# A longer GpSimd operation between slot writes, and gathered rows turned through the scratch in list order

## The chip, the core and the metric

The kernel runs on one NeuronCore of a Trainium2 chip. Its engines run beside each other, each with an instruction stream of its own: TensorE (PE in the rows; PEld is its weight load), VectorE (DVE), ScalarE (ACT), GpSimd (POOL) and SyncE (SP), which issues most of the DMAs. GpSimd issues the DMAs whose rows are picked by an index, gathers and scatters. The metric is device time in microseconds (us) of one execution, the median of several.

## What is computed

Windowed causal attention over 8 batches, 8 heads, 576 positions and head size 64, whose output rows are the input of a mixture of experts with the top 2 of 8 experts per row.

```python
scores = scale * q @ k.T                       # window of 64 positions, causal
attn = softmax(where(mask, scores, -1e9))
x = (attn @ v).transpose(0, 2, 1, 3).reshape(4608, 512)
noisy = x @ w_gate + log1p(exp(x @ w_noise)) * noise
top2 = the two largest of 8 per row; w = softmax over these two
for e in range(8):                             # rows whose top 2 holds e
    h = maximum(x[mask] @ w1[e], 0)            # 512 -> 1024
    out[mask] += w[mask, e] * (h @ w2[e])      # 1024 -> 512
```

## The kernel before

**Attention.** The 36 units `j` (128 rows each) run in one software pipeline, `for j in range(NT + 3)` (L719 to 769), in which the steps of neighbouring units are woven together by hand. Among them are `pv` (L324, 64 small matmuls of 64x85 per unit), the four transposes of `transp` (L301), and on GpSimd the softmax subtraction (L289). Each unit's output rows are stored to `X` (`xrows`) in DRAM.

**Routing.** After units 7, 14, 21, 27 and 36 a `route(c)` (L407) works out for the rows so far which two experts they go to and at which place of each expert's list. Then `scatter` (L481) writes, for each unit and each of the two choices, 128 entries of 8 bytes (row number, weight) to `L` (`slots`) in DRAM: one indirect DMA of GpSimd (L483). There are 72 of these slot writes. Ahead of each stands a one-element memset of `spacer` (L482). They are queued in the list `slots` and drained by `drain_slots` at fixed places of the program: one to three per unit within the attention loop, several at a time behind it.

**Experts.** For each expert `e` the list is cut into chunks of 384, 448 and 384 rows, `(e, c)`. `load_list` (L520) and `load_lists` (L532) read the lists back from `slots` with SP, once all slot writes ahead of them have landed. `gather` (L543) fetches the rows of a chunk with one indirect DMA per tile of 128 rows (L546, tile `xg`). `turn` (L564) brings them into the layout that TensorE needs, with the feature on the partition, and splits them into a high and a low part, `xh` (ACT, L584) and `xl` (DVE, L585). `up` (L609) multiplies by `w1` (L625 to 627, 96 matmuls per chunk) and `down` (L645) by `w2` (L654 to 656, 24 matmuls per tile); `add_rows` (L640) adds the weighted result to the output with an indirect DMA of GpSimd.

For expert 0 the turning is done by TensorE transposes (L579). For experts 1 to 7 it goes through a scratch `xs` in DRAM: per tile one DMA out (`turn_out`, L555, pieces of 128 values) and one back (`turn_in`, L560), each partition then holding 4 whole blocks of 128 values, and a 32x32 block transpose on DVE (L574) into `xy`. In `xy` the row number within a tile is laid out such that L584 and L585 read with a stride (`"p t k c -> p k c t"`) and write in sequence.

**What sets the order.** `spread` (L55) lays a list of side tasks evenly over the groups of matmuls of a chunk. The gather of the next chunk (`whole` for all tiles, then `turn_out` for all tiles, then `turn_in` for all tiles) is laid over `up` of the current one, the turn of the next chunk over `down` of the current one. Each engine and SP's queue run their instructions in this written order. The first matmuls of chunk (0, 0), `up00`, are issued ahead of time within the last units of the attention loop. Chunk (0, 1) is gathered after the first four routings, chunk (0, 2) after the last.

Of the kernel before, what the change touches and what calls it, by code (L numbers as in the profile page):

```python
# [8 lines left out]
F32 = mybir.dt.float32  # L9
# [5 lines left out]
OP = mybir.AluOpType  # L15
# [6 lines left out]
NT = NP * NB  # L22
# [13 lines left out]
W1G = 12  # L36
TURN = 33
AHEAD = 16
XB = 8
SLOTS = 5  # L40
WARM = 4

# [23 lines left out]
def tile_kernel(ctx, tc, qT, kT, vx, vT, wgx, noise, w1, w2, out):  # L66
    nc = tc.nc
# [68 lines left out]
    warm(10)  # L136
    ident = consts.tile([128, 128], F32)
    make_identity(nc, ident)
    spacer = consts.tile([1, 1], F32)
    zero = gw.tile([128, DM], F32, name="zero", bufs=1)  # L140
    nc.vector.memset(zero, 0.0)

# [264 lines left out]
    def route(c):  # L407
# [71 lines left out]
        yield lambda: nc.vector.reciprocal(w[:, 0, :, 1], sm)  # L479
        yield lambda: nc.vector.tensor_tensor(w[:, 1, :, 1], e, w[:, 0, :, 1], op=OP.mult)  # L480
        def scatter(c2, q):  # L481
            nc.gpsimd.memset(spacer, 0.0)  # L482
            s = nc.gpsimd.indirect_dma_start(  # L483
                out=L, out_offset=bass.IndirectOffsetOnAxis(ap=posi[:, c2, q:q + 1], axis=0),
                in_=val[:, c2, q, :], in_offset=None)
            for x in scattered:
                tc.declare_no_dep(s.ins, x.ins, reason="distinct slots")
            scattered.append(s)
# [21 lines left out]
    pending, slots = [], []  # L510


    LT, XG, XH, XL, HH = {}, {}, {}, {}, {}
    work = [(e, c) for e in range(E) for c in range(len(CHUNKS))]

    def tiles(c):
        return [(q, min(128, CHUNKS[c] - q * 128)) for q in range(-(-CHUNKS[c] // 128))]
# [25 lines left out]
    def gather(e, c):  # L543
        def whole(q, m):
            XG[e, c, q] = exa.tile([128, DM], F32, name="xg", bufs=XB)
            nc.gpsimd.indirect_dma_start(out=XG[e, c, q][:m], out_offset=None, in_=X[:DUMP + seen.get((e, c), NT) * 128],  # L546
                                         in_offset=bass.IndirectOffsetOnAxis(ap=LT[e, c][q][:m, 0:1], axis=0))
        if e == 0:
            return [lambda q=q, m=m: whole(q, m) for q, m in tiles(c)]

        b = {}

        def turn_out(q, m):
            b[q] = dram.tile([4, 128, 128], F32, name="xs", bufs=8)
            nc.sync.dma_start(b[q].rearrange("g p c -> (g p c)")[:m * DM].rearrange("(g p c) -> p g c", g=4, c=128),  # L555
                              XG[e, c, q][:m].rearrange("p (g c) -> p g c", g=4))

        def turn_in(q, m):
            XG[e, c, q] = exa.tile([128, DM], F32, name="xg", bufs=XB)
            nc.sync.dma_start(XG[e, c, q][:, :m * 4],  # L560
                              b[q].rearrange("g p c -> (g p c)")[:m * DM].rearrange("(p x) -> p x", p=128))
        return [lambda q=q, m=m, f=f: f(q, m) for f in (whole, turn_out, turn_in) for q, m in tiles(c)]

    def turn(e, c):  # L564
        pool = (exa, EXB.get("p"))[work.index((e, c)) % 2]
# [5 lines left out]
        def f(q, m):  # L571
            if e:
                y = exa.tile([128, m // 32, KD, 32], F32, name="xy", bufs=2)
                nc.vector.transpose(y.rearrange("p t k c -> p (t k c)"), XG[e, c, q][:, :m * 4])  # L574
                cur[q] = y.rearrange("p t k c -> p k c t")
            else:
                y = turn_bank()[:, :KD * m].rearrange("p (k m) -> p k m", k=KD)
                for k in range(KD):
                    nc.tensor.transpose(y[:, k], XG[e, c, q][:m, k * 128:k * 128 + 128], ident[:m, :m])  # L579
                cur[q] = y.rearrange("p k (c t) -> p k c t", c=32)  # L580

        def g(q, m):
            h, l = (x[:, :, q * 128:q * 128 + m].rearrange("p k (c t) -> p k c t", c=32) for x in (xh, xl))
            nc.scalar.activation(h, cur[q], AF.Copy)  # L584
            nc.vector.tensor_tensor(l, cur[q], h.bitcast(F32), op=OP.subtract)  # L585
        return [lambda q=q, m=m, x=x: x(q, m) for q, m in tiles(c) for x in (f, g)]
# [341 lines left out]
```

## Time and profile before

| | |
|---|---|
| median of 3 runs | 1135.25 us (1126.39 to 1136.22) |
| the profiled execution | 1131.99 us, its span 1130.2 us |
| PE busy | 1044.2 us (92%) |
| DVE, ACT, POOL busy | 469.2, 437.4, 338.6 us |
| slot writes, POOL L483 | 72, mean 972 ns |
| gathers, POOL L546 | 80; those of experts 1 to 7 mean 990 ns |

The profile is of one execution, with times from the start of the span. An engine's row has its start, its duration, the line, the operation, the tiles (written <- read) and in brackets how long the engine was idle ahead of it and what ended that. "issue" there means that the profile shows nothing that the engine waited for, "remote" that the releaser is not known. PEclk is the granted share of TensorE's full clock: 1.00 is 2.4 GHz and 0.50 is 1.2 GHz.

### The profile page before, as it was taken

To read this page: it belongs to the slowest core of one execution; us is meant where nothing else is said; L and a number is where in the kernel's file an instruction comes from. 1 tells how busy PE (TensorE), PEld (TensorE's weight loads), DVE (VectorE), ACT (ScalarE), POOL (GpSimd) and SP (SyncE) were. 2 spreads that over 40 slices of the span, in tenths; PEclk is the share of its full clock that TensorE was granted. 3 is DMA by queue.
4 is the path that set the end of the run, shared out by engine and by line. 5 is a ranking of instruction groups with operands and counts; after the bars stand their busy time and mean duration, and the time that the engine had idled before them with its cause. 6 is when DMAs were issued, how large, how long until landed. Compare 5 with 4: busy or idle time off the path is not lost. (4 is left out here: it accounts for less than half of the span.)

```text
span 1130.2 us, 19820 instructions
## 1 busy us (share of the span) xinstructions
PE 1044.2 (92%) x8025; PEld 925.7 (82%) x8025; DVE 469.2 (42%) x943; ACT 437.4 (39%) x1011; POOL 338.6 (30%) x387
## 2 busy tenths in 40 slices
PE   9788888578599999999999999999999999999996
PEld 8777777366589888898988898889888988889895
DVE  5586556324114523452263325334533452354320
ACT  4776555332123432442253335323432343253320
POOL 4345444616412222122312123212221222322121
PEclk9898888879699999999999999999999999999998
DMA  9988889537414752564447445634762564244422
GB/s 321 314 300 206 214 198 307 150 133 235 123 27 112 221 146 33 173 195 103 81 130 200 103 108 146 180 81 98 203 172 40 157 205 113 44 99 112 102 33 31
DMA packets 104519, 168.07 MB, mean 149 GB/s; under 512 B 15096, under 2 KB 50530, under 8 KB 102626
## 3 DMA queue, kind: packets, MB, share of 16 engines
q1 hardware_dynamic: 84962, 126.78, 35.3%
q0 software_dynamic: 19456, 39.93, 19.2%
q8 instruction: 65, 1.06, 0.4%
q14 instruction: 36, 0.29, 0.1%
HBM read 109.54 MB, written 57.14 MB: 147 GB/s over the span
## 5 line engine op out<-in xcount | busy, mean ns | idle before, releaser
L625 PE MATMUL ps_u<-xh,w1h 128*128 128x384 f32 (+1 forms) x752 | 261.6, 348 | 15.6 <-ACT xh L584 15.1
L640 POOL DMA_INDIRECT out_dram<-yo,lts x70 | 112.1, 1602 | 543.9 <-ACT yo L659 430.7
L626 PE MATMUL ps_u<-xl,w1h 128*128 128x384 f32 (+1 forms) x752 | 261.4, 348 | 4.5 <-DVE xl L585 4.5
L627 PE MATMUL ps_u<-xh,w1l 128*128 128x384 f32 (+1 forms) x752 | 260.3, 346 | 0.0
L654 PE MATMUL ps_d<-w2h,hh 128*128 128x512 f32 x576 | 225.3, 391 | 0.0
L656 PE MATMUL ps_d<-w2h,hl 128*128 128x512 f32 x576 | 225.2, 391 | 0.0
L655 PE MATMUL ps_d<-w2l,hh 128*128 128x512 f32 x576 | 225.0, 391 | 0.0
L632 DVE SCALAR_TENSOR_TENSOR hl<-ps_u,hh 128x384 fp32r<-128x384 f32 x188 | 104.8, 557 | 275.9 <-ACT hh L631 261.6
L631 ACT ACTIVATE hh<-ps_u 128x384 fp32r<-128x384 f32 x188 | 92.5, 492 | 246.9 <-PE ps_u L627 236.5
L625 PEld LDWEIGHTS ps_u<-xh,w1h 128*128 128x128 f32 x752 | 141.9, 189 | 23.9 <-ACT xh L584 18.7
L626 PEld LDWEIGHTS ps_u<-xl,w1h 128*128 128x128 f32 x752 | 141.9, 189 | 11.2 <-DVE xl L585 6.7
L627 PEld LDWEIGHTS ps_u<-xh,w1l 128*128 128x128 f32 x752 | 141.9, 189 | 4.0
L585 DVE TENSOR_TENSOR xl<-xy,xh 128x512 fp32r<-128x512 f32 (+1 forms) x70 | 71.5, 1021 | 150.7 <-ACT xh L584 150.7
L654 PEld LDWEIGHTS ps_d<-w2h,hh 128*128 128x128 f32 x576 | 108.6, 189 | 23.8 <-issue 1.8
L656 PEld LDWEIGHTS ps_d<-w2h,hl 128*128 128x128 f32 x576 | 108.4, 188 | 22.8
L655 PEld LDWEIGHTS ps_d<-w2l,hh 128*128 128x128 f32 x576 | 108.5, 188 | 21.9
L659 ACT ACTIVATE yo<-ps_d,lts 128x512 f32<-128x512 f32 x63 | 43.4, 690 | 160.2 <-PE ps_d L656 119.1
L324 PE MATMUL ps_o<-vw,pt 64*64 64x85 f32 x2176 | 71.0, 257 | 29.4 <-issue 22.8
L584 ACT ACTIVATE xh<-xy 128x512 fp32r<-128x512 f32 (+1 forms) x70 | 74.4, 1063 | 56.1 <-DVE xy L574 56.1
L324 PEld LDWEIGHTS ps_o<-vw,pt 64*64 64x64 f32 x2176 | 58.7, 149 | 40.3 <-issue 32.1
L483 POOL DMA_INDIRECT slots<-val,posi x72 | 70.0, 972 | 20.1 <-issue 14.7
L546 POOL DMA_INDIRECT xg<-xrows,lts x70 | 69.3, 990 | 21.4 <-issue 20.1
(149 smaller groups left out, 991.3 us busy)
## 6 DMA issues: line engine op xcount, KB each, us to landing
xs<-xg SPq DMA_DIRECT2D x63, 256.0 KB
xg<-xs SPq DMA_DIRECT2D x63, 256.0 KB
w2s<-in_w_dram SPq DMA_DIRECT2D x7, 2048.0 KB
w1s<-in_w_dram SPq DMA_DIRECT2D x7, 2048.0 KB
vw<-in_vx_dram SPq DMA_DIRECT2D x36, 272.0 KB
out_dram<-zero SPq DMA_DIRECT2D x37, 256.0 KB
qc<-in_qT_dram SPq DMA_DIRECT2D x36, 256.0 KB
KW<-in_kT_dram SPq DMA_DIRECT2D x36, 256.0 KB
```

The source lines that it names most:

```text
L324: nc.tensor.matmul(PO[j][u * 64:u * 64 + 64, a, g * 2 + x, :], lhsT=pt[pa, w, u * 2 + g, x * 64:x * 64 + 64], rhs=v[pa, (i + w) % 2, :, u, ...
L584: nc.scalar.activation(h, cur[q], AF.Copy)
L585: nc.vector.tensor_tensor(l, cur[q], h.bitcast(F32), op=OP.subtract)
L625: nc.tensor.matmul(p[:, :n], lhsT=w1h[:, k, fs], rhs=xh[:, k, :n], start=(k == 0), stop=False)
L626: nc.tensor.matmul(p[:, :n], lhsT=w1h[:, k, fs], rhs=xl[:, k, :n], start=False, stop=False)
L627: nc.tensor.matmul(p[:, :n], lhsT=w1l[:, k, fs], rhs=xh[:, k, :n], start=False, stop=(k == KD - 1))
L631: nc.scalar.activation(h, p[:, :main], AF.Relu)
L632: nc.vector.scalar_tensor_tensor(l, p[:, :main], 0.0, h.bitcast(F32), op0=OP.max, op1=OP.subtract)
L640: nc.gpsimd.indirect_dma_start(out=out[:DUMP + seen.get((e, c), NT) * 128], out_offset=bass.IndirectOffsetOnAxis(ap=LT[e, c][q][:m, 0:1], ...
L654: nc.tensor.matmul(p, lhsT=hh[f][:, sl], rhs=w2h[:, f, :], start=(f == 0), stop=False)
L655: nc.tensor.matmul(p, lhsT=hh[f][:, sl], rhs=w2l[:, f, :], start=False, stop=False)
L656: nc.tensor.matmul(p, lhsT=hl[f][:, sl], rhs=w2h[:, f, :], start=False, stop=(f == KF - 1))
```

## The change

Two parts. First, `spacer` grows to 256 values, and ahead of those slot writes that are issued from unit 34 on (`j < NT - 2` no longer holds), the one-element memset is replaced by an addition of 256 values on one partition, also on GpSimd. That concerns 39 of the 72 slot writes. Second, for experts 1 to 7 the gathered tiles go to the scratch `xs` as whole rows (2 KB each), the scratch is one tile per chunk, and it is read back by four DMAs per chunk, one for each group of 32 partitions, in pieces of 128 values, into one tile `xc` (one buffer). DVE's block transpose then gives `xy` in list order, and L584 and L585 (L588 and L589 of the change) read runs of 32 values. The pool `xg` shrinks from 8 buffers to 5, since the way back no longer uses it.

```diff
+PAUSE = 256
-XB = 8
+XB = 5
...
-    spacer = consts.tile([1, 1], F32)
+    spacer = consts.tile([1, PAUSE], F32)
...
         def scatter(c2, q):
-            nc.gpsimd.memset(spacer, 0.0)
+            if j < NT - 2:
+                nc.gpsimd.memset(spacer[:, 0:1], 0.0)
+            else:
+                nc.gpsimd.tensor_tensor(spacer, zero[0:1, :PAUSE], zero[0:1, :PAUSE], op=OP.add)
             s = nc.gpsimd.indirect_dma_start(
...
-        b = {}
+        b = dram.tile([WIDE, DM], F32, name="xs", bufs=3)
 
         def turn_out(q, m):
-            b[q] = dram.tile([4, 128, 128], F32, name="xs", bufs=8)
-            nc.sync.dma_start(b[q].rearrange("g p c -> (g p c)")[:m * DM].rearrange("(g p c) -> p g c", g=4, c=128),
-                              XG[e, c, q][:m].rearrange("p (g c) -> p g c", g=4))
-
-        def turn_in(q, m):
-            XG[e, c, q] = exa.tile([128, DM], F32, name="xg", bufs=XB)
-            nc.sync.dma_start(XG[e, c, q][:, :m * 4],
-                              b[q].rearrange("g p c -> (g p c)")[:m * DM].rearrange("(p x) -> p x", p=128))
-        return [lambda q=q, m=m, f=f: f(q, m) for f in (whole, turn_out, turn_in) for q, m in tiles(c)]
+            nc.sync.dma_start(b[q * 128:q * 128 + m], XG[e, c, q][:m])
+
+        def turn_in(g):
+            if g == 0:
+                XC[e, c] = exa.tile([128, WIDE // 32, 128], F32, name="xc", bufs=1)
+            nc.sync.dma_start(XC[e, c][32 * g:32 * g + 32, :CHUNKS[c] // 32],
+                              rows(b, g * 128, [[DM, 32], [32 * DM, CHUNKS[c] // 32], [1, 128]]))
+        return ([lambda q=q, m=m, f=f: f(q, m) for f in (whole, turn_out) for q, m in tiles(c)]
+                + [lambda g=g: turn_in(g) for g in range(4)])
...
-                nc.vector.transpose(y.rearrange("p t k c -> p (t k c)"), XG[e, c, q][:, :m * 4])
-                cur[q] = y.rearrange("p t k c -> p k c t")
+                nc.vector.transpose(y.rearrange("p t k c -> p (t k c)"), XC[e, c][:, q * 4:q * 4 + m // 32].rearrange("p t d -> p (t d)"))
+                cur[q] = y.rearrange("p t k c -> p k t c")
...
         def g(q, m):
-            h, l = (x[:, :, q * 128:q * 128 + m].rearrange("p k (c t) -> p k c t", c=32) for x in (xh, xl))
+            h, l = (x[:, :, q * 128:q * 128 + m].rearrange("p k (t c) -> p k t c", c=32) for x in (xh, xl))
```

GpSimd, the last units of the attention loop, before (`val`, `posi` are the entries and places of a routing; DMASW counts GpSimd's own DMAs):

```order
L483 DMA slots<-val_172,posi 38400x2 [waits DMASW2_49]
L482 MEMSET spacer 1x1 [waits Pool_49]
L483 DMA slots<-val_172,posi 38400x2 [waits DMASW3_49]
L289 TENSOR_TENSOR t<-t,mx 128x512 [waits DVE_49,Activation_49]
L482 MEMSET spacer 1x1 [waits Pool_49]
L483 DMA slots<-val_172,posi 38400x2 [waits DMASW4_49]
```

and the same place of the change:

```order
L487 DMA slots<-val_172,posi 38400x2 [waits DMASW2_49]
L484 MEMSET spacer 1x1 [waits Pool_49]
L487 DMA slots<-val_172,posi 38400x2 [waits DMASW3_49]
L290 TENSOR_TENSOR t<-t,mx 128x512 [waits DVE_49,Activation_49]
L486 TENSOR_TENSOR spacer<-zero 1x256 [waits Pool_49]
L487 DMA slots<-val_172,posi 38400x2 [waits DMASW4_49]
```

Nothing has moved on GpSimd; from this place on the memset's place is taken by the addition, 39 times. SP's queue, from the reading of the lists to the second chunk of expert 1, before:

```order
L535 DMA lts<-slots 64x7x2
L209 DMA w1s<-in_w_dram 128x4096
L555 DMA xs<-xg 128x4x128 x3
L560 DMA xg<-xs 128x512 x3
L209 DMA w1s<-in_w_dram 128x4096
L555 DMA xs<-xg 128x4x128 x3
L555 DMA xs<-xg 64x4x128
L560 DMA xg<-xs 128x512 x3
L560 DMA xg<-xs 128x256
L213 DMA w2s<-in_w_dram 128x4096
```

and of the change:

```order
L539 DMA lts<-slots 64x7x2
L210 DMA w1s<-in_w_dram 128x4096
L558 DMA xs<-xg 128x512 x3
L563 DMA xc<-xs 32x12x128 x4
L210 DMA w1s<-in_w_dram 128x4096
L558 DMA xs<-xg 128x512 x3
L558 DMA xs<-xg 64x512
L563 DMA xc<-xs 32x14x128 x4
L214 DMA w2s<-in_w_dram 128x4096
```

The places are the same; a chunk's way back is always four DMAs now, and each of them carries rows of all tiles of the chunk. DVE at the turn of chunk (1, 1), before (DMAHW counts SP's DMAs):

```order
L574 STREAM_TRANSPOSE xy<-xg 128x512 [waits DMAHW0_49]
L585 TENSOR_TENSOR xl<-xy,xh 128x4x128 [waits Activation_49]
L574 STREAM_TRANSPOSE xy<-xg 128x512 [waits DMAHW1_49]
L585 TENSOR_TENSOR xl<-xy,xh 128x4x128 [waits Activation_49]
L574 STREAM_TRANSPOSE xy<-xg 128x512 [waits DMAHW2_49]
```

and of the change:

```order
L578 STREAM_TRANSPOSE xy<-xc 128x512 [waits DMAHW3_49,DMAHW4_49,DMAHW2_49,DMAHW1_49]
L589 TENSOR_TENSOR xl<-xy,xh 128x4x128 [waits Activation_49]
L578 STREAM_TRANSPOSE xy<-xc 128x512
L589 TENSOR_TENSOR xl<-xy,xh 128x4x128 [waits Activation_49]
L578 STREAM_TRANSPOSE xy<-xc 128x512
```

The first transpose of a chunk now waits for all four loads, the others for none.

## Rows read from the trace of the kernel before

**Rows 1.** Stretches of 2 us and one of 100: length, busy time per engine, PEclk, DMA share, GB/s

```profile
228.00:230.00 2.00, 0.58 (x2) 0.18 (x2) 0.00 (x0) 0.00 (x0) 1.74 (x4) 0.50 0.02 1
268.00:270.00 2.00, 2.00 (x11) 1.65 (x10) 0.00 (x0) 0.00 (x0) 1.78 (x3) 1.00 0.95 385
296.00:298.00 2.00, 2.00 (x7) 1.79 (x7) 1.39 (x6) 0.00 (x0) 1.59 (x1) 0.50 0.97 336
500.00:600.00 100.00, 99.33 (x487) 88.72 (x486) 39.84 (x67) 36.89 (x65) 25.93 (x20) 1.00 0.48 121
```

**Rows 2.** PE in order of time: start us, duration us, instruction [idle before <- releaser]

```profile
105.36 0.27 PE L324 MATMUL ps_o<-vw,pt 64*64 64x85 f32 x1 [0.44 <-issue]
107.53 1.09 PE L324 MATMUL ps_o<-vw,pt 64*64 64x85 f32 x42 [0.34 <-issue]
...
211.55 0.96 PE L324 MATMUL ps_o<-vw,pt 64*64 64x85 f32 x39
235.54 0.69 PE L627 MATMUL ps_s<-xh,w1l 128*128 128x384 f32 x1 [0.22 <-issue]
237.40 0.69 PE L625 MATMUL ps_s<-xh,w1h 128*128 128x384 f32 x1 [1.17 <-DVE hl L632]
...
279.03 0.39 PE L656 MATMUL ps_d<-w2h,hl 128*128 128x512 f32 x1
294.52 0.74 PE L625 MATMUL ps_u<-xh,w1h 128*128 128x448 f32 x1 [15.10 <-ACT xh L584]
...
406.19 0.36 PE L625 MATMUL ps_u<-xh,w1h 128*128 128x448 f32 x1
```

**Rows 3.** POOL in order of time, in the same places

```profile
105.87 0.96 POOL L483 DMA_INDIRECT slots<-val,posi  x1 [0.23 <-issue]
...
208.59 1.06 POOL L483 DMA_INDIRECT slots<-val,posi  x1 [0.15 <-issue]
231.46 0.96 POOL L483 DMA_INDIRECT slots<-val,posi  x1 [0.22 <-issue]
254.39 1.37 POOL L546 DMA_INDIRECT xg<-xrows,lt  x1 [21.97 <-issue]
265.22 1.01 POOL L483 DMA_INDIRECT slots<-val,posi  x1 [5.37 <-DVE val L480]
288.73 0.96 POOL L483 DMA_INDIRECT slots<-val,posi  x1 [0.23 <-issue]
```

**Rows 4.** ACT in order of time: after its long wait, and in chunk (1, 0)

```profile
293.51 0.69 ACT L659 ACTIVATE yo<-ps_d,lt 128x512 f32<-128x512 f32 x1 [12.07 <-remote]
...
395.56 0.69 ACT L659 ACTIVATE yo<-ps_d,lts 128x512 f32<-128x512 f32 x1 [2.67 <-PE ps_d L656]
```

**Rows 5.** Groups of instructions by form: count | busy us, mean ns of one | idle before

```profile
L584 ACT ACTIVATE xh<-xy 128x512 fp32r<-128x512 f32 x63 | 71.1, 1128 | 56.1 <-DVE xy L574 56.1
L585 DVE TENSOR_TENSOR xl<-xy,xh 128x512 fp32r<-128x512 f32 x63 | 68.4, 1085 | 146.9 <-ACT xh L584 146.9
L289 POOL TENSOR_TENSOR t<-t,mx 128x512 f32<-128x512 f32 x36 | 37.6, 1044 | 96.8 <-DVE mx L288 96.2 <-issue 0.5
L217 POOL TENSOR_TENSOR w1l<-w1s,w1h 128x256 fp32r<-128x256 f32 x16 | 11.4, 732 | 8.6 <-ACT w1h L216 8.6
L482 POOL MEMSET spacer<- 1x1 f32 x72 | 7.0, 97 | 0.1
L585 DVE TENSOR_TENSOR xl<-ps_u,xh 128x512 fp32r<-128x512 f32 x6 | 4.2, 692 | 32.6 <-ACT xh L584 21.8 <-issue 10.8
L584 ACT ACTIVATE xh<-ps_u 128x512 fp32r<-128x512 f32 x6 | 3.6, 597 | 8.3 <-PE ps_u L579 5.5 <-PE ps_d L656 2.3 <-issue 0.4
```

**Rows 6.** Waits: engine, line <- releaser: us in total, times, longest us

```profile
PE ps_u L626 <- DVE xl L585: 4.5, 7, 0.7
```

**Rows 7.** SP's queue in order of time: start us, duration us, DMA issue

```profile
251.18 0.40 SPq L525 DMA_DIRECT2D lt<-slots  x1
...
388.05 2.12 SPq L560 DMA_DIRECT2D xg<-xs  x4
```

**Rows 8.** DVE in order of time, first and last of the turn of chunk (1, 1)

```profile
391.03 0.70 DVE L574 STREAM_TRANSPOSE xy<-xg 128x512 f32<-128x512 f32 x1
...
402.17 0.43 DVE L585 TENSOR_TENSOR xl<-xy,xh 128x256 fp32r<-128x256 f32 x1 [0.54 <-ACT xh L584]
```

More of the change, by code (lines that the diff above doesn't have):

```diff
@@ L510, in tile_kernel @@
     pending, slots = [], []
-    LT, XG, XH, XL, HH = {}, {}, {}, {}, {}
+    LT, XG, XC, XH, XL, HH = {}, {}, {}, {}, {}, {}
     work = [(e, c) for e in range(E) for c in range(len(CHUNKS))]
@@ L579, in f @@
                     nc.tensor.transpose(y[:, k], XG[e, c, q][:m, k * 128:k * 128 + 128], ident[:m, :m])
-                cur[q] = y.rearrange("p k (c t) -> p k c t", c=32)
+                cur[q] = y.rearrange("p k (t c) -> p k t c", c=32)
         def g(q, m):
-            h, l = (x[:, :, q * 128:q * 128 + m].rearrange("p k (c t) -> p k c t", c=32) for x in (xh, xl))
+            h, l = (x[:, :, q * 128:q * 128 + m].rearrange("p k (t c) -> p k t c", c=32) for x in (xh, xl))
             nc.scalar.activation(h, cur[q], AF.Copy)
```

## The prediction

> **What bounds the kernel now.** I read the stretches first. From 360 us to the end the kernel is TensorE: busy 99.33 of 100 us at full clock [rows 1]. What the change could win there is at most the missing 0.7%. So I looked for holes in PE, and the ones that count stand between 212 and 300 us, where the attention loop ends and expert 0 begins.
>
> Hole A: 39 small matmuls of one `pv` begin at 211.55 and last 0.96 us; the next steps come one by one, and PE is free again only at 237.40 [rows 2]. In between it is busy 0.58 of 2 us, its clock falls to 1.2 GHz, ACT and DVE do nothing, and the DMA engines are at 0.02 [rows 1]. No semaphore holds PE ("issue" is named as releaser). What does run is GpSimd: 19 slot writes back to back, from 208.59 to 232.42, one every (231.46 - 208.59)/18 = 1.27 us [rows 3], of which 0.96 us is the write and 0.31 us the memset with its gaps.
>
> Hole B: the last matmul of `down` (0, 0) ends at 279.42; the first of chunk (0, 1) starts at 294.52, after 15.1 us [rows 2]. It waits for ACT's last `xh`, which stands behind an ACT instruction that was idle for 12.07 us up to 293.51 [rows 4]. That instruction needs PE's matmuls of 279.42 and nothing later: the news of them took 14 us. Again GpSimd issues slot writes all the while, 265.22 to 289.69, and adds one output tile behind them [rows 3]. After hole B the clock is still 1.2 GHz until about 300: 7 matmuls in 2 us [rows 1].
>
> That the two belong together shows in a small case too. Of three writes in a row the last ends at 106.83; PE, which had been let through one matmul at a time, goes on with 42 of them at 107.53 [rows 2, 3]. So a write holds PE back for about its own length, with a lag of 0.7 us. Against it speaks 268 to 270 us: dense writes as well, and PE is busy all of the time with large matmuls [rows 1]. The obstruction hits streams of short instructions and the messages of PE to others, not long matmuls that already run.
>
> Is it the DMA engines? The Trainium skill, page "DMA: Bandwidth & Descriptors", section "Issuing engines are not separate DMA queues", has all issuers share the same 16 DMA engines; by it spreading the same writes over more time would free nothing that is short. The share of 0.02 in the midst of hole A speaks against that.
>
> **The pause.** 39 slot writes get an addition of 256 values in place of the memset: 2 in the loop, 19 in the run of hole A, 18 in that of hole B. No row shows it. The two nearest are 732 ns for 256 values and 1044 ns for 512, both on 128 partitions; the memset it replaces took 97 ns, which is the lower end [rows 5]. I take 0.65 us, near the row of the same length. (The Trainium skill, "GPSIMD Engine Reference", section "Elementwise — side-by-side cycle accounting", gives about 2.6 cycles per value for two inputs; that is an estimate of 0.56 us, and by it each run below would end about 2 us earlier.) The period becomes 1.27 - 0.09 + 0.65 = 1.83 us, of which 0.87 us is free of writes instead of 0.31.
>
> Run A then ends at 208.59 + 18 x 1.83 + 0.96 = 242.5 instead of 232.4. Behind its last write wait the list of chunk (0, 1) and its gathers. Today SP reaches that list at 251.18 and the first gather follows at 254.39 [rows 3, 7]; by the new run the list can go at about 244.5 (2 us for landing) and the gathers from 247.7 to 253. Run B can start then, and with one output add among its 18 writes it ends at about 253 + 18 x 1.83 + 1.9 = 288, about where it ends today (289.7). So the longer runs cost nothing at their ends, as long as PE gets through hole A sooner.
>
> **Hole A.** From 212.5 to 237.4 PE does some 25 small matmuls, four transposes and six large matmuls, with one ACT and one DVE step between: about 3.3 us of work at the pace of their neighbours. If PE is free for 0.87 of each 1.83 us, that takes about 7 us. Gain 24.9 - 7 = 18 us. `down` (0, 0) then needs its first gathered tile at about 254.5; its gather starts at 247.7 and should be in by 251. No new wait.
>
> **Hole B.** With gaps of 0.87 us PE's message should arrive within one or two periods. I leave 2 us of the 15.1: gain 13. The 5.9 us at half clock after it cost 3 us; gain 3. Chunk (0, 1) would start at about 294.5 - 34 = 260.5.
>
> **What is given back.** Run B now lies over `up` (0, 1), whose ACT and DVE steps wait for PE's messages. Nothing shows what that costs; between nothing and half of the 25 us, I allow 5.
>
> **Experts 1 to 7.** Bytes and matmuls stay. L584 and L585 read runs in place of a stride. Where they read in sequence today (from PSUM, expert 0) the same size takes 597 and 692 ns, against 1128 and 1085 [rows 5]. That is 63 x 0.53 + 63 x 0.39 = 58 us of ACT and DVE work, nearly all under PE. What surfaces is the wait for the last `xl` at the start of each expert, 4.5 us in 7 times [rows 6]. A turn of three tiles gets 2.8 us shorter, more than the 0.7 each: gain 4.5. Not moved: `xg` with 5 buffers, since each tile is written out before its buffer comes round.
>
> The new wait: DVE's first transpose needs all four loads, and the first load needs all tiles written out. In the tightest kind, chunk (e, 1), the loads are issued 388.05 to 390.17 and the turn runs from 391.03 to 402.60, PE needing it at 406.19 [rows 2, 7, 8]. The four loads start when the last tile has landed and have 448 pieces each, so I put the first transpose 3 us later, at 394. Four tiles at 0.70 + 0.60 + 0.69 + 0.2 = 2.2 us end near 402. Behind the waiting transpose stand only DVE's and ACT's own turn steps and ACT's first output copy, which today runs at 395.56 [rows 4]. Cost nothing, covered by 4 us.
>
> **The sum.** 18 + 13 + 3 - 5 + 4.5 = 33.5 us off 1131.99 is 1098.5; I say 1100. That execution is 0.3% under the median of 1135.25, well within the spread of the three.
>
> **The rivals.**
> *The gaps don't help (slower).* If PE is held for as long as a run lasts, whatever the gaps, it is free 5 us after the last write, as now: 247.5 instead of 237.4, which is 10 later. Run B starts 10 later at 275 and ends at 310; PE starts chunk (0, 1) at about 315, 20 later than now, with 4.5 won back: 1132 + 16 = 1148. For it speaks that PE crawled on to 235.54, 3 us after the last write, with GpSimd at rest; against it the quick recovery at 107.53 [rows 2]. This is also what the page's rule on shared DMA engines would give. It decides from a hold per write above 1.83 us; from (236 - 208.6)/19 I read 1.44.
> *Only hole A closes (no change that can be measured).* If messages come through only after the run, chunk (0, 1) starts 4.8 us after the last write of run B, as now: 288 + 4.8 = 292.8, 1.7 us sooner; with 4.5 it is 1126.
> *The turn comes late.* If the loads take 5 us more than I think, PE waits about 1 us and more in seven chunks, and with slow pieces 3 us: 20 us given back, 1120.
> *Everything closes.* No loss under run B and no remainder: 1090.
>
> **How the numbers follow.** My forecast (1090 to 1112) gets 0.58, "only A" 0.18, "gaps don't help" 0.14, the late turn 0.10. The measurement tells about 1%, 11 us, from no change. Faster by more than 1%, below about 1124: 0.58 + 0.08 of the late turn + 0.03 of "only A" = 0.69. Within 1%: 0.17. Slower by more than 1%: 0.14. For 8 in 10 the range goes from 1088 (more closes than I think) to 1138, which leaves out the slower rival and little else. The likeliest case's own range is 1090 to 1112.
>
> **What would show it.** In the changed profile: additions on GpSimd of about 0.65 us, writes 1.8 us apart; PE's `pv` of 211.55 through by about 220, the half clock of 215 to 243 mostly gone; ACT idle under 3 us where it was 12.07; L584 and L585 of experts 1 to 7 at about 0.6 and 0.7 us; DVE's first transpose of a middle chunk waiting for `xc` about 3 us. I am wrong if PE still crawls at one step per 0.7 us between spaced writes, if ACT's long wait still ends after the last write, or if PE waits for `xh` in the middle chunks.

## The result

The changed kernel takes 1093.98 us (median of 4 runs, 1092.77 to 1099.71) against 1133.38 us for the kernel before on the same chip (4 runs). The ratio is 0.967, with a 95% interval of 0.961 to 0.973. The forecast was 1100.0 us, range 1088 to 1138, "faster" with 0.69.

The profiled execution of the changed kernel took 1092.84 us, with a span of 1091.0 us (before: 1130.2). Its lines number differently: the pause is L486, the slot write L487, the gather L550, the turn's transpose L578, `xh` L588, `xl` L589, the matmuls of `up` L629 to L631, those of `down` L658 to L660, the output add L644.

**Hole A.** PE in order of time, the answer to [rows 2] (start us, duration us, instruction [idle before <- releaser]):

```profile
212.69 2.54 PE L325 MATMUL ps_o<-vw,pt 64*64 64x85 f32 x64
...
218.05 0.44 PE L629 MATMUL ps_s<-xh,w1h 128*128 128x384 f32 x1 [1.17 <-DVE hl L636]
...
235.72 0.39 PE L658 MATMUL ps_d<-w2h,hh 128*128 128x512 f32 x1
...
260.83 0.39 PE L660 MATMUL ps_d<-w2h,hl 128*128 128x512 f32 x1
262.28 0.47 PE L629 MATMUL ps_u<-xh,w1h 128*128 128x448 f32 x1 [1.05 <-ACT xh L588]
```

All 64 matmuls of the `pv` go in one stretch. The matmul that waits for `hl`, at 237.40 before, starts at 218.05. **Hole B** is in the last two rows: the wait for `xh` is 1.05 us where it was 15.10, and chunk (0, 1) starts at 262.28, before at 294.52.

GpSimd in order of time, as [rows 3]: the first and last write of run A, the first gather, the first and last write of run B, the first gather of chunk (0, 2):

```profile
209.26 0.98 POOL L487 DMA_INDIRECT slots<-val,posi  x1 [0.16 <-issue]
242.38 1.25 POOL L487 DMA_INDIRECT slots<-val,posi  x1 [0.16 <-issue]
248.48 0.98 POOL L550 DMA_INDIRECT xg<-xrows,lt  x1 [4.86 <-issue]
...
253.97 1.02 POOL L487 DMA_INDIRECT slots<-val,posi  x1 [0.17 <-issue]
285.81 0.98 POOL L487 DMA_INDIRECT slots<-val,posi  x1 [0.16 <-issue]
...
295.02 1.01 POOL L550 DMA_INDIRECT xg<-xrows,lt  x1 [0.30 <-issue]
```

The writes mostly stand 1.77 us apart. What stood behind ACT's long wait of [rows 4]: the last message of `down` (0, 0) now comes as soon as its matmul has ended.

```profile
261.26 0.69 ACT L663 ACTIVATE yo<-ps_d,lt 128x512 f32<-128x512 f32 x1 [2.08 <-PE ps_d L660]
```

Stretches, as [rows 1] (length, busy time of PE, PEld, DVE, ACT and POOL, PEclk, DMA share, GB/s). At 228 PE is busy all of the time at full clock; at 263, behind the start of chunk (0, 1), the clock is still at half; at 268, in run B, PE loses nothing; and from 500 on it is busy 100.00 of 100 us where it was 99.33.

```profile
228.00:230.00 2.00, 2.00 (x14) 2.00 (x13) 1.02 (x4) 1.29 (x7) 1.78 (x4) 1.00 0.40 137
263.00:265.00 2.00, 2.00 (x6) 1.35 (x6) 1.04 (x4) 0.00 (x0) 1.81 (x3) 0.50 0.89 364
268.00:270.00 2.00, 2.00 (x12) 1.81 (x11) 0.36 (x2) 0.69 (x2) 1.76 (x3) 1.00 0.06 17
500.00:600.00 100.00, 100.00 (x496) 89.88 (x494) 36.85 (x66) 32.45 (x64) 25.81 (x20) 1.00 0.55 134
```

Groups by form, as [rows 5], and two waits, as [rows 6] (waiter <- releaser: us in total, times, longest us). `xh` and `xl` of experts 1 to 7 cost 629 and 693 ns in place of 1128 and 1085, the pause 626 ns in the mean. DVE now waits for the loads of `xc`, which costs PE nothing, and PE waits 1.3 us for the gather of chunk (0, 2).

```profile
L588 ACT ACTIVATE xh<-xy 128x512 fp32r<-128x512 f32 x63 | 39.6, 629 | 98.6 <-DVE xy L578 98.6
L589 DVE TENSOR_TENSOR xl<-xy,xh 128x512 fp32r<-128x512 f32 x63 | 43.7, 693 | 117.6 <-ACT xh L588 116.9 <-issue 0.7
L486 POOL TENSOR_TENSOR spacer<-zero 1x256 f32<-1x256 f32 x39 | 24.4, 626 | 1.0
```

```profile
DVE xy L578 <- DMA xc<-xs: 45.8, 10, 7.2
PE ps_u L583 <- DMA xg<-xrows,lt: 1.5, 2, 1.3
```

**Where the 39.2 us of span come from.** PE's first matmul of each part, in both traces:

| first matmul of | before, us | changed, us | sooner by |
|---|---|---|---|
| `up` (0, 0) | 209.75 | 210.46 | -0.7 |
| `down` (0, 0) | 256.55 | 235.72 | 20.8 |
| `up` (0, 1) | 294.52 | 262.28 | 32.2 |
| `down` (0, 1) | 317.43 | 284.21 | 33.2 |
| `up` (0, 2) | 338.86 | 307.12 | 31.7 |
| `down` (0, 2) | 355.61 | 323.90 | 31.7 |
| `up` (2, 0) | 478.89 | 446.45 | 32.4 |
| last `down` | 1102.74 | 1063.24 | 39.5 |

So hole A gave 21.5 us, hole B 11.4, the clock behind it 1.0; run B took 1.5 back, and experts 1 to 7 gave 7.8; less the 0.7 us by which `up` (0, 0) starts later, that is 39.5. These are two single executions: in the traces of all kernels with the same attention loop `up` (0, 0) starts between 207.9 and 218.4 us, so lengths between two of these points are safer to compare than the points themselves.

### The profile page after: what moved, and what is told of

It reads as the page before. It is cut to its first block, busy times and chain, and to the rows that moved or that the text cites. A ratio compares the mean times of both kernels' runs of the same rounds, so it can differ in the third digit from the quotient of the medians.

```text
span 1091.0 us, 19873 instructions
## 1 busy us (share of the span) xinstructions
PE 1034.9 (95%) x8025; PEld 922.8 (85%) x8025; DVE 447.2 (41%) x943; ACT 403.1 (37%) x1011; POOL 359.8 (33%) x387
## 5 line engine op out<-in xcount | busy, mean ns | idle before, releaser
L644 POOL DMA_INDIRECT out_dram<-yo,lts x70 | 111.3, 1590 | 537.6 <-ACT yo L663 384.3
L629 PE MATMUL ps_u<-xh,w1h 128*128 128x384 f32 (+1 forms) x752 | 260.3, 346 | 2.2 <-DVE hl L636 1.1
L631 PE MATMUL ps_u<-xh,w1l 128*128 128x384 f32 (+1 forms) x752 | 260.0, 346 | 0.0
L658 PE MATMUL ps_d<-w2h,hh 128*128 128x512 f32 x576 | 225.3, 391 | 0.0
L660 PE MATMUL ps_d<-w2h,hl 128*128 128x512 f32 x576 | 225.0, 391 | 0.0
L629 PEld LDWEIGHTS ps_u<-xh,w1h 128*128 128x128 f32 x752 | 141.6, 188 | 8.0 <-ACT xh L588 1.8
L631 PEld LDWEIGHTS ps_u<-xh,w1l 128*128 128x128 f32 x752 | 141.5, 188 | 4.0
L658 PEld LDWEIGHTS ps_d<-w2h,hh 128*128 128x128 f32 x576 | 108.5, 188 | 24.2 <-issue 2.2
L659 PEld LDWEIGHTS ps_d<-w2l,hh 128*128 128x128 f32 x576 | 108.5, 188 | 22.9 <-DVE w2l L218 0.9
L660 PEld LDWEIGHTS ps_d<-w2h,hl 128*128 128x128 f32 x576 | 108.4, 188 | 22.6
L589 DVE TENSOR_TENSOR xl<-xy,xh 128x512 fp32r<-128x512 f32 (+1 forms) x70 | 46.6, 666 | 121.1 <-ACT xh L588 120.4
L588 ACT ACTIVATE xh<-xy 128x512 fp32r<-128x512 f32 (+1 forms) x70 | 42.5, 608 | 101.8 <-DVE xy L578 101.8
L550 POOL DMA_INDIRECT xg<-xrows,lts x70 | 70.6, 1009 | 21.3 <-issue 21.0
L487 POOL DMA_INDIRECT slots<-val,posi x72 | 71.4, 991 | 12.8 <-issue 12.5
```

Of the source, the lines that this page charges most:

```text
L487: s = nc.gpsimd.indirect_dma_start(out=L, out_offset=bass.IndirectOffsetOnAxis(ap=posi[:, c2, q:q + 1], axis=0), in_=val[:, c2, q, :], in_ ...
L629: nc.tensor.matmul(p[:, :n], lhsT=w1h[:, k, fs], rhs=xh[:, k, :n], start=(k == 0), stop=False)
L631: nc.tensor.matmul(p[:, :n], lhsT=w1l[:, k, fs], rhs=xh[:, k, :n], start=False, stop=(k == KD - 1))
L644: nc.gpsimd.indirect_dma_start(out=out[:DUMP + seen.get((e, c), NT) * 128], out_offset=bass.IndirectOffsetOnAxis(ap=LT[e, c][q][:m, 0:1], ...
L658: nc.tensor.matmul(p, lhsT=hh[f][:, sl], rhs=w2h[:, f, :], start=(f == 0), stop=False)
L659: nc.tensor.matmul(p, lhsT=hh[f][:, sl], rhs=w2l[:, f, :], start=False, stop=False)
```

## The experiments

The kernels are compared with the kernel before, run on the same chip beside them; the two probes compute nothing of the reference and are compared stage by stage. The first four ran on one chip, the next four on a second, `probe` and `pause_mixed` on a third, `probe2` and `pause_fourth` on a fourth. That will matter.

**1. The two parts alone.** `pause_only` is the kernel before with the spacer's edit; `layout_only` is the changed kernel with the memset back:

```
-            if j < NT - 2:
-                nc.gpsimd.memset(spacer[:, 0:1], 0.0)
-            else:
-                nc.gpsimd.tensor_tensor(spacer, zero[0:1, :PAUSE], zero[0:1, :PAUSE], op=OP.add)
+            nc.gpsimd.memset(spacer[:, 0:1], 0.0)
```

> The kernel before with the pause alone; gathered rows come back as before. Theory (the gaps close both holes; the new way back only takes the waits at the start of experts 1 to 7): from the starts of up and down in the two traces the pauses are worth 20.8 us at the start of down (0, 0) and 31.7 us at the start of down (0, 2), and the rest of the 39.2 us, 7.6, comes one expert at a time; so 1133.4 - 31.7 = 1102, ratio 0.972, wait of PE for the last xl still there 7 times. Rival (the new way back thins what the DMA engines do and has a part in closing the holes): above 1110, or a hole of over 5 us left at 212 to 240 or at 262.

> The changed kernel without the pause: the memset is back in all 72 writes, the way back of the gathered rows is the new one. Theory: both holes as before (down (0, 0) at 256 us, up (0, 1) at 294 us), and 7.6 us off at experts 1 to 7, 1.1 us in each of experts 2 to 7: 1126, ratio 0.993. Rival 1 (the new way back costs time that the changed kernel hides elsewhere): 1133 or more. Rival 2 (it has a part in closing the holes): under 1115.

Measured: `pause_only` 1103.83 us, ratio 0.976 (0.970 to 0.982); `layout_only` 1126.94 us, ratio 0.994 (0.991 to 0.997), with the before at 1135.52. Both are clear of the noise, the second under 2%. The two gains are 31.7 and 8.6 us; their sum is 40.3, and both edits together gave 39.4. In `pause_only` both holes are closed (25.4 us from the start of `up` (0, 0) to that of `down` (0, 0), and 1.05 us of waiting for `xh`), and PE still waits 7 times for the last `xl`, 4.6 us in all. In `layout_only` both holes are still there: 46.5 us from `up` to `down`, then a wait of 12.3 us, in which ACT waits for PE's last message until run B is over. Its last write ends at 298.02:

```profile
299.03 0.69 ACT L660 ACTIVATE yo<-ps_d,lt 128x512 f32<-128x512 f32 x1 [9.33 <-remote]
```

Within the spread of the runs the parts add up: the pause closes the holes, the new way back works in experts 1 to 7.

**2. One hole at a time.** In the changed kernel the pause is kept in the first 21 of its 39 writes (`pause_a`), or in the last 18 (`pause_b`):

```
-            if j < NT - 2:
+            if j < NT - 2 or len(scattered) >= 54:     (pause_a)
+            if len(scattered) < 54:                    (pause_b)
```

> The changed kernel with the pause in 21 writes only (2 in the loop, 19 of run A); the 18 writes of run B get the memset again, one every 1.27 us from about 254 to 278. Theory of a hold per write (messages are late as long as writes come densely): PE goes through hole A as in the changed kernel, down (0, 0) starts at 235.7, and the first matmul of chunk (0, 1), due at 262.3, comes some 4 us after the last write, at about 283: 21 us later than in the changed kernel; 1114. Rival (messages are late by a fixed 14 us, as they were in the kernel before): first matmul at 276, total 1107. Rival (hole B was only a consequence of hole A, by where run B fell): no wait over 3 us, total 1094.

> The changed kernel with the pause in the 18 writes of run B only; the 21 before them have the memset. Theory (each run makes its own hole): hole A as before, PE crawls from 212.5 to 237.4 and down (0, 0) starts at 256.5; run B then starts at about 265 and takes 32 us, without a wait of over 3 us for chunk (0, 1), which starts at about 282; total 1094 + 20.5 = 1114. Rival (the holes trade places, a late start of run B costs elsewhere): above 1122. Rival (hole A is not made by the writes): no gain against the kernel without any pause, 1126.

Measured (one run each): `pause_b` 1114.52 us, where the theory had 1114: hole A is open (46.8 us from `up` to `down`), and there is no hole B behind it. That the total fits to half a microsecond is luck, since `down` (0, 0) starts at 261.19 and `up` (0, 1) at 285.39, 4.7 and 3.4 us later than expected. `pause_a` took 1100.77 us, and none of the three expectations fits: hole A is closed, and chunk (0, 1) starts at 271.82, which is 9.5 us later than in the changed kernel, not 21 and not 14. The messages are late, by 3.1 to 3.8 us from the end of the matmul to the start of the ACT instruction that needs it. ACT's waits for them, and GpSimd's row that follows:

```profile
264.41 0.60 ACT L588 ACTIVATE xh<-ps_u 128x512 fp32r<-128x512 f32 x1 [4.28 <-remote]
270.81 0.69 ACT L663 ACTIVATE yo<-ps_d,lt 128x512 f32<-128x512 f32 x1 [5.80 <-remote]
```

```profile
271.85 0.95 POOL L487 DMA_INDIRECT slots<-val,posi  x1 [0.64 <-DMA slots<-val,posi]
```

Two things differ from hole B of before. This dense run had begun at 255.95, only 5 to 11 us ahead of the matmuls whose messages count, against 14 us there (265.22 [rows 3], 279.42 [rows 2]); and GpSimd itself paused, behind the output add and for earlier writes to land (0.64 to 1.41 us). So a dense run makes a hole of its own, here a shallower one. Whether that comes from the shorter time that the run had been going on or from GpSimd's pauses, this run does not separate. My theory had neither.

**3. The length of the pause.** The changed kernel with `PAUSE` 64, 128 and 512:

> The changed kernel with additions of 64 values: by the line from 97 ns for 1 value to 600 ns for 256 an addition takes 0.22 us, the writes come every 1.39 us, 0.41 us of it free. Theory 1 (a write holds PE for about 1.44 us, as the prediction read): no free time is left, hole A and hole B stay, down (0, 0) starts near 256; about 1120 to 1126. Theory 2 (it is the free stretch between two writes that counts, and one of 0.31 us is just too short): PE gets most of its steps through; under 1105.

> The changed kernel with additions of 128 values, 0.35 us each: a write every 1.52 us, 0.54 us of it free. Theory 1 (a hold of 1.44 us): PE is free 0.08 of 1.52 us, it still crawls in hole A; about 1112. Theory 2 (the free stretch counts): both holes closed, the runs end 5 us sooner than with 256 values, the 1.3 us that PE waits for the gather of chunk (0, 2) goes; 1092.

> The changed kernel with additions of 512 values, about 1.1 us each: a write every 2.27 us. Both theories: both holes closed. What the longer runs cost: run A ends 9 us later than in the changed kernel, at 252, the gathers of chunk (0, 1) come at 257 to 262, and PE waits for them about 6 us; run B ends 304 + 6, the gathers of chunk (0, 2) follow 8 us behind, and PE waits there for about 12 us more; 1093 + 18 = 1111. Rival (GpSimd's end has slack): under 1098.

Measured: 1100.31, 1091.22 and 1117.07 us (one run each, so 1091.22 is not told apart from the changed kernel's 1092.77 to 1099.71). The additions took 0.294, 0.399 and 1.051 us in the mean. Periods below are those that most writes of a run have:

| kernel | a write every, us | free of it, us | `up` (0, 0) to `down` (0, 0), us |
|---|---|---|---|
| before | 1.27 | 0.31 | 46.8 |
| `PAUSE` 64 | 1.46 | 0.48 | 38.6 |
| `PAUSE` 128 | 1.57 | 0.59 | 28.7 |
| changed (256) | 1.77 | 0.79 | 25.3 |
| `PAUSE` 512 | 2.20 | 1.22 | 25.9 |

At 1.46 us per write more than half of hole A is left, at 1.57 little, at 1.77 none; hole B is closed with the shortest pause already (PE waits 1.05 us for `xh` at 64 and at 128). The times are those of theory 2 at both lengths (under 1105, and 1092). Theory 1, the hold of 1.44 us per write that the prediction read off the run, falls: at 128 values it left PE 0.08 us per write and 1112 us. As the writes themselves last the same in all these runs, they cannot tell the period from the free stretch. Too long a pause costs at the run's end: with 512 values PE waits 15.4 us in two places for the gathers of chunks (0, 1) and (0, 2), where I had expected 18. With 128 the runs end earlier, and the 1.3 us for chunk (0, 2) are gone.

**4. What of a slot write is it?** `probe` puts a stream of short matmuls beside 24 operations of one kind per stage.

```
+            if kind in ("write", "write_gap", "write_memsets"):
+                free(nc.gpsimd.indirect_dma_start(out=S[q], out_offset=at, in_=val, in_offset=None))
...
+            elif kind == "read":
+                nc.gpsimd.indirect_dma_start(out=got[:, i], out_offset=None, in_=S[q], in_offset=at)
```

> A kernel that computes nothing of the reference; the output stays zero. 11 stages between barriers; in each TensorE does 128 matmuls of 64x85, then 8 turns of one matmul and one ACT copy that wait for each other, then 8 matmuls of 128x512, while another engine issues 24 DMAs or additions: none; writes of 8 bytes per partition to DRAM, one every 1.27 us (as the dense runs); the same with the addition of 256 values between (1.77 us); reads of 8 bytes, dense; writes with 64 rows instead of 128, dense; additions alone; writes with five memsets between; reads of 2 KB per row, dense; plain DMAs issued by GpSimd; plain DMAs issued by SP; and the dense writes again. Theory 1 (the issuing of an indirect DMA on GpSimd, whatever it moves, takes away what PE needs to go on): dense writes and dense reads of 8 bytes both stretch the 128 matmuls by more than 3 times against the stage with none, the writes with a pause by under 1.3 times, additions alone not at all, memsets as a pause as little as the addition. Theory 2 (it is the small writes on their way into DRAM): dense writes do, dense reads don't, and plain DMAs of the same 8-byte rows from SP do as well. Theory 3 (it is the number of rows): half the rows make the stage with writes as quick as with a pause, though they come as densely.

PE in order of time, the 128 matmuls of each stage (256 rows, since each shows as two). The stages in order: none; dense writes; writes with the addition; dense reads of 8 bytes; 64 rows; additions alone; memsets as a pause; reads of 2 KB. Of the crawl only its first and last rows are shown.

```profile
60.06 36.52 PE L139 MATMUL ps_a<-one,ball 64*64 64x85 f32 x256 [60.06 <-ACT ball L136]
122.59 9.75 PE L139 MATMUL ps_a<-one,ball 64*64 64x85 f32 x67 [5.05 <-ACT ball L136]
132.57 0.30 PE L139 MATMUL ps_a<-one,ball 64*64 64x85 f32 x1 [0.23 <-issue]
133.28 0.54 PE L139 MATMUL ps_a<-one,ball 64*64 64x85 f32 x2 [0.42 <-issue]
...
152.27 24.90 PE L139 MATMUL ps_a<-one,ball 64*64 64x85 f32 x174 [0.42 <-issue]
203.80 36.53 PE L139 MATMUL ps_a<-one,ball 64*64 64x85 f32 x256 [5.11 <-ACT ball L136]
266.20 9.66 PE L139 MATMUL ps_a<-one,ball 64*64 64x85 f32 x64 [5.11 <-ACT ball L136]
...
295.69 25.52 PE L139 MATMUL ps_a<-one,ball 64*64 64x85 f32 x179 [1.80 <-issue]
347.60 8.47 PE L139 MATMUL ps_a<-one,ball 64*64 64x85 f32 x58 [5.11 <-ACT ball L136]
...
376.98 26.65 PE L139 MATMUL ps_a<-one,ball 64*64 64x85 f32 x187 [1.80 <-issue]
429.77 36.53 PE L139 MATMUL ps_a<-one,ball 64*64 64x85 f32 x256 [5.11 <-ACT ball L136]
491.94 36.52 PE L139 MATMUL ps_a<-one,ball 64*64 64x85 f32 x256 [5.11 <-ACT ball L136]
553.74 13.01 PE L139 MATMUL ps_a<-one,ball 64*64 64x85 f32 x90 [5.11 <-ACT ball L136]
```

Undisturbed, the 256 rows take 36.5 us, in the first stage at a PEclk of 1.00 and in the later ones at 0.50 alike. Dense writes make it 54.6, dense reads 55.0, half the rows 56.0, reads of 2 KB 51.6, and the repeat of the dense writes at the end 54.6. With the addition or five memsets between, and beside additions alone, it is 36.5: nothing lost. So theory 2 (small writes into DRAM) and theory 3 (the number of rows) fall; what holds PE back comes with GpSimd's indirect DMAs one behind the other, whichever way the data go, and a stretch of about 0.8 us without one lifts it, whether an addition or memsets fill it. Whether it is their issuing or what follows from it (the crawl outlives the last write) the stages do not separate. My "more than 3 times" was too much: the crawl begins only 14 us after the first write (118.47 to 132.57; for 2 KB reads 17.5) and ends 3.6 us after the last (148.66 to 152.27). In the kernel before it begins sooner. The first of the three writes that end at 106.83 [rows 3] is this one, and PE takes single steps from 105.36 on [rows 2], 2 us later; in hole A they begin 4 us after the first write of run A. So 14 us is no fixed delay, and what sets it no run shows.

```profile
103.32 0.99 POOL L483 DMA_INDIRECT slots<-val,posi  x1 [0.15 <-issue]
```

In the crawl PE is busy 3.73 of 19 us, and the DMA engines 0.02 of it (same columns as the stretches above):

```profile
133.00:152.00 19.00, 3.73 (x14) 2.33 (x14) 0.00 (x0) 0.00 (x0) 13.05 (x25) 0.50 0.02 1
```

Two stages tell nothing: the 24 plain DMAs took GpSimd 13.6 us and SP 12.4, shorter than the 14 us after which the crawl begins here. So whether plain DMAs do the same is open. The turns between PE and ACT came when the dense runs were over, so the late messages were not measured by themselves.

**5. Better versions.** `pause_all` has the addition behind all 72 writes (`if j < 0:`), `pause_mixed` behind all, in two lengths:

```
+            n = 192 if len(scattered) < 54 else 96
+            nc.gpsimd.tensor_tensor(spacer[:, :n], zero[0:1, :n], zero[0:1, :n], op=OP.add)
```

> The changed kernel with the addition behind all 72 slot writes, the 33 of the attention loop before it too. There 1 to 3 writes come per step, and PE waits 20.4 us in 46 times at the matmuls of L325 without a semaphore. Theory (each dense pair or triple makes a small hole): these waits fall to under 5 us; as each step of the loop is also held by ACT and DVE, half of that reaches the end, 1085. Rival (GpSimd's softmax subtraction stands behind the pauses, 0.5 us each in each step): the loop gets longer, down (0, 0) later than 236; 1098 or more.

> All 72 slot writes with an addition, of 192 values up to run A and of 96 in run B. Additions of 0.50 and 0.34 us (by the line through 294, 399 and 626 ns for 64, 128 and 256). Theory (free stretches of about 0.68 us are enough for PE in the loop and in run A, and 0.5 us for the long matmuls beside run B; shorter runs take away what PE waits for gathers, 2.9 us for chunk (0, 1) and 1.6 us for chunk (0, 2) with 256 values in all): 1085 - 4 = 1081. Rival (0.68 us is short of what hole A needs, as 0.58 us was with 128 values, where down (0, 0) came 3.4 us later after up (0, 0)): 1087.

Measured: `pause_all` 1085.39 us, ratio 0.957 (0.952 to 0.963); `pause_mixed` 1079.66 us, ratio 0.953 (0.947 to 0.959) on another chip. The interval of `pause_mixed` lies below the changed kernel's (0.961 to 0.973), that of `pause_all` just touches it; between the two they overlap. The pairs and triples of the attention loop did make small holes: in `pause_all` `up` (0, 0) starts at 203.68 (changed: 210.46) and `down` (0, 0) at 220.09 (235.72). PE's waits without a semaphore at the `pv` matmuls, in the changed kernel and in `pause_all`:

```profile
PE ps_o L325 <- issue: 20.4, 46, 3.3
```

```profile
PE ps_o L325 <- issue: 15.5, 18, 3.3
```

They fall from 46 to 18 in number, but by 4.9 us only, and not under 5 us as I had expected; so the total of 1085 came out right, and not by these waits alone. Of the 18, some stand beside the three gathers of chunk (0, 0), which are dense indirect DMAs too: the gathers begin at 169.55, and PE takes steps of 0.7 us from 170.88 to 173.80. Others are there without any crawl: on the chip of part 6, where nothing is held back, 13 of them make 20.2 us.

**6. Backlog or hold?** The last pair was to tell whether a pause behind every fourth write does.

```
-            if j < NT - 2:
+            if j < NT - 2 or len(scattered) % 4:     (pause_fourth, PAUSE = 512)
```

> The stages of the probe again (it computes nothing of the reference, the output stays zero), with writes of 8 bytes per partition only: none; 24 dense; 24 with additions of 16, 32, 64, 96, 128 values between, by the line through the additions seen 1.38, 1.41, 1.46, 1.51 and 1.56 us apart; 24 with an addition of 512 values behind every fourth (1.51 us on average) and behind every eighth (1.38), and two of them behind every eighth (1.51); 8, 12 and 16 dense. In the probe PE went on 3.9 us after the last of 24 dense writes, as if each took 1.27 + 3.9/24 = 1.43 us of something that falls behind; and it began to crawl 14 us after the first write. Theory 1 (a backlog of 0.16 us per dense write, felt from some 11 writes on): 8 dense writes cost PE nothing, 12 under 3 us, 16 some 6 us; a pause behind every fourth write costs nothing, two behind every eighth nothing, one behind every eighth little; spaced evenly, the loss falls towards nothing between 1.38 and 1.46 us. Theory 2 (each write holds PE for 1.43 us, and only a free stretch behind it lets PE on): with the pause behind every fourth write PE gets on in every fourth gap only and loses more than half of what it loses beside dense ones (15 us); 8 dense writes cost about 8 x 0.9 = 7 us.

> The changed kernel with an addition of 512 values (1.05 us) behind every fourth of the last 39 slot writes, and the memset behind the others: 1.51 us per write on average. Theory 1 (a backlog that a longer pause now and then works off): both holes closed, the runs end 5 us sooner than in the changed kernel, 1092. Theory 2 (each write needs its own pause): hole A mostly open, down (0, 0) after 245; above 1104.

Neither theory could be tested, for a reason that was a large surprise. On this chip the dense writes disturb nothing. `probe2`'s second stage is `probe`'s dense one: the same instructions, a write every 1.27 us, the last of them

```profile
148.57 0.96 POOL L121 DMA_INDIRECT s<-val,pos  x1 [0.22 <-issue]
```

and PE beside it, in the stage with none and in the dense stage:

```profile
61.23 36.52 PE L127 MATMUL ps_a<-one,ball 64*64 64x85 f32 x256 [61.23 <-ACT ball L124]
123.50 36.52 PE L127 MATMUL ps_a<-one,ball 64*64 64x85 f32 x256 [5.05 <-ACT ball L124]
```

All 13 stages take 36.5 us. The kernel before took 1079.17 us there (13 runs, 1071.62 to 1081.18), against 1124.2 to 1143.4 in all of its runs on the other chips. `pause_fourth` took 1071.16 us, ratio 0.994 (0.991 to 0.996): as much as `layout_only` gained elsewhere. That where nothing holds PE back the pauses neither gain nor cost is likely from this, but the new way back was not run alone there. If the chips differ in nothing else, which no run shows, the 55 us between 1079 and 1135 are what the obstruction costs the kernel before, and `pause_mixed`, at 1079.66 on a chip with it, still loses some 8.5 us against the 1071.16 here. What sets the chips apart no trace here shows. GpSimd's durations and periods are the same.

## Why the prediction was right

**Right in its cause, in part by luck in its sum.** Both holes came from dense slot writes and closed with the pause; `pause_only`, `pause_b` and `layout_only` show it one by one. The picture of a hold was wrong: the prediction let each write hold PE for about its own length, so that PE works in the gaps, but with spaced writes PE is not held at all, and the `pv` goes in one stretch of 2.54 us across them. The sum was 33.5 us and the traces give 39.5: three terms were 10.3 us too small, two 3.6 us too large, and `up` (0, 0) started 0.7 us later, so the errors cancelled in part. Term by term:

- *Pause*: 0.65 us forecast, 0.626 measured, period 1.77 for 1.83. The list went at 245.26 (244.5), the gathers at 248.48 to 253.2 (247.7 to 253), run B ended at 286.8 (288). By the figure of the Trainium skill, "GPSIMD Engine Reference", section "Elementwise — side-by-side cycle accounting", the estimate was 0.56 us; most of these additions took 0.60.
- *Hole A*: 18 forecast, 21.5 measured. The matmul at 237.40 came 19.4 us sooner, which with the later start of `up` (0, 0) makes 20.1; the other 1.4 are, on balance, the half clock that had stayed on behind the hole in the kernel before, which I had counted for hole B alone.
- *Hole B*: 13 forecast, 11.4 measured. The wait itself fell by 14 us, to 1.05. But `down` (0, 0) takes 25.5 us where it took 22.9: coming sooner, it waits longer for the routing's `sc` and `cum` (1.18 and 2.15 us, where PE had stood 0.55 and 1.68), for a part of `w2` (0.49) and ahead of two transposes of gathered tiles (0.23 and 0.39). The stretch at half clock behind the routing was there before too. A part that starts earlier finds its producers where they were.
- *Clock behind hole B*: 3 forecast, 1.0 measured. The stretch at 263 us is still at half clock. I took the whole of it as won.
- *Given back under run B*: 5 forecast, 1.5 measured, and in another place. Through the whole of `up` (0, 1), 262.3 to 284.2, PE is busy without a gap; what run B costs is that the gather of chunk (0, 2) can only go behind its end, and comes 1.3 us too late. The 5 us had no row behind them.
- *Experts 1 to 7*: 4.5 forecast, 7.8 measured. The step that was too small took the wait of 0.64 us from [rows 6] as all there was. The bound set ahead of it was wrong as well: the missing 0.7% of PE's busy share is about 5 us from 360 us to the end, and more than that was won. The start of expert 2, before and changed:

```profile
478.47 0.39 PE L656 MATMUL ps_d<-w2h,hl 128*128 128x512 f32 x1
478.89 0.45 PE L625 MATMUL ps_u<-xh,w1h 128*128 128x384 f32 x1
479.99 0.45 PE L626 MATMUL ps_u<-xl,w1h 128*128 128x384 f32 x1 [0.65 <-DVE xl L585]
```

```profile
446.22 0.39 PE L660 MATMUL ps_d<-w2h,hl 128*128 128x512 f32 x1
446.45 0.33 PE L629 MATMUL ps_u<-xh,w1h 128*128 128x384 f32 x1
446.62 0.34 PE L630 MATMUL ps_u<-xl,w1h 128*128 128x384 f32 x1
```

From start to start the second step took 1.10 us and takes 0.17; the first took 0.42 and takes 0.23. That is 0.93 + 0.19 = 1.12 us, where the list of waits shows 0.65: it counts from the modelled end of a matmul, and this one is drawn 0.45 us long though the next could start 0.17 us behind it. With 0.1 us for the matmul behind, 1.2 us in each of experts 2 to 7 and 0.5 in expert 1 make the 7.8.

- *The turn in the middle chunks*: DVE's first transpose was to come 3 us later, under 4 us of cover. At chunk (1, 1) it starts at 364.95, on the clock of before (32.24 us more) at 397.2, which is 6.2 us later than 391.03 [rows 8]; the turn ends at 372.35, and PE needs it at 373.95. It stayed hidden with 1.6 us to spare. The answer was right by luck of the margin; the estimate was half of what it is.

```profile
364.95 0.71 DVE L578 STREAM_TRANSPOSE xy<-xc 128x512 f32<-128x512 f32 x1 [6.08 <-DMA xc<-xs]
```

**The rivals.** "The gaps don't help" was to decide at a hold above 1.83 us per write. Hole A closes between 1.46 and 1.77 us per write, so it was wrong, but not by much: a pause of 64 values left more than half of hole A open. "Only hole A closes" fell with the wait of 1.05 us for chunk (0, 1), and "the turn comes late" with the 1.6 us to spare. "Everything closes" (1090) came nearest, 4 us off, nearer than the forecast itself.

The Trainium skill, "DMA: Bandwidth & Descriptors", section "Issuing engines are not separate DMA queues", has the DMAs of all issuers run on the same 16 DMA engines. The rival that the prediction drew from it, that spacing frees nothing, does not describe this stall: the trace shows it at a DMA share of 0.02 in the kernel and in the probe.

**What is shown and what is not.** Shown: GpSimd's indirect DMAs, issued back to back, make PE take short instructions a few at a time, and 0.6 to 0.8 us without one between them lifts all or nearly all of it, in the kernel on three chips and in the probe on one of these. Shown in the kernel only: that PE's messages come late. Argued only: that something falls behind by a little per DMA and overflows. The crawl's start 14 us into a run of the probe and `pause_a` fit that, the start 2 to 4 us into a run in the kernel before does not without a further cause; the pair that was to test it met a chip without the effect. Open: whether plain DMAs do it too, what inside the chip is shared, and why one of four chips doesn't show it.

## What to carry to other kernels

Where an engine waits for nothing that the profile shows ("issue"), or a message comes long after the work it reports, look at what runs back to back on the other engines, GpSimd's indirect DMAs first; a pause of about 0.6 us between them is nearly free if nobody waits for their end, and the right length is the shortest that closes the hole. This rests on one kernel. Price a wait from start to start of the instructions around it, not by its idle time. And measure a change of this kind on more than one chip: here the pause alone is worth 32 us on the one chip where it was run alone, kernels with it gained on three, and on a fourth a kernel with it gained no more than the new way back does by itself elsewhere.

## What was not expected of the hardware

- A dense run of 24 indirect DMAs costs a stream of short matmuls 15 to 19.5 us on one chip. The writes of 8 bytes among them cost 18.1 us there and 0.0 on another, with the same period of 1.27 us on GpSimd.
- In the probe the stall starts late: 14 us after the first DMA of a dense run, and for reads of 2 KB 17.5 us. In the kernel before it starts after 2 to 4 us. It outlives the run, by 3.6 us in the probe's dense writes.
- In the crawl PE's instructions mostly start 0.7 us or a multiple of it apart (132.57, 133.28, then 135.41), whatever the DMAs move.
